# Top-k attention and gated feed-forward: scores split at 320 columns, attention areas in the outer banks, waits between different banks declared needless, feed-forward paced by section

## The chip, the cores and the metric

One core of one Trainium2 chip. The metric is the device time of the program in microseconds (us); the time before is the median of three runs. The profile comes from one further execution, and its span (first to last instruction of the program) is a little shorter than that execution's time.

The engines are named as in the profile: PE (TensorE matmuls) with PEld (its weight loads), DVE (VectorE), ACT (ScalarE), POOL (GpSimd), SP (SyncE, which here issues DMAs). Each runs its own queue in order, and an instruction waits on semaphores that other engines raise. PSUM, into which PE writes, is divided into banks of 512 fp32 columns for each of 128 partitions.

## The reference, cut to what matters

```python
def _attn_ref(q, k, v):                      # (8, 8, 576, 64) each
    scores = scale * np.matmul(q, k.transpose(0, 1, 3, 2))
    kth = np.partition(scores, -32, axis=-1)[..., -32:-31]
    scores = np.where(scores >= kth, scores, -1e9)
    attn = np.exp(scores - np.max(scores, axis=-1, keepdims=True))
    attn = attn / (np.sum(attn, axis=-1, keepdims=True) + 1e-09)
    return np.matmul(attn, v)

def _moe_ref(x, w_in, conv_w, w_out):        # x: (8, 576, 512), d_ff 1024
    h = np.maximum(x @ w_in, 0.0)
    conv_out = sum(conv_w[k] * hp[:, k:k + S, :] for k in range(3))   # hp: h padded by a row
    gate = 1.0 / (1.0 + np.exp(-conv_out))
    return h * gate @ w_out
```

## The kernel before, in words

The work is 288 tiles of 128 score rows by 576 columns. A batch has four pairs of heads; a pair has four full row blocks (one tile for each of its two heads) and a tail block in which the last 64 rows of both heads share a tile, so nine tiles, 36 a batch. The rows of a batch are done in two sections: section 0 takes two row blocks and the tail of every pair (20 tiles), section 1 the other two (16 tiles). When a section's attention is done, its feed-forward is queued and runs among the tiles of the next section: eight `Expand` units (x by w_in, each 12 matmuls, 258 columns wide for section 0 and 322 for section 1, L431), a convolution on POOL, a tanh on ACT, a gate on DVE, then `Contract` units (12 matmuls of 512 columns, L581).

`iteration(it)` records one step of a software pipeline, and each engine's queue is in that order (`manual_schedule`). On PE: four transposes of the weights of tile it-5 (L326), feed-forward matmuls (L431, L581) as a budget allows, a tail transpose (L339), the scores of a row block every second step (L241, or L229 for a tail block), and the products with v (`av`, L357 and L360). On ACT: relu of an expand (L445), the sign pass `sides` (L288), the copy of scores out of PSUM (`evacuate`, L248), the copy of an attention area (`av_out`, L368), the copy of the transposes (L331), the exponential of tile it-3 into `e_ps` (L300), and a tanh if there is one (L492). On DVE: seven partial maxima (L255), the merging of candidates (L275, L277), a maximum (L303), `select` (L307, tile `hot`), sometimes a gate (L500) and the row sums' inverses (L373, L374), and `weigh` (L313), which reads `e_ps`.

Two PSUM tiles matter. `s_ps` has three banks (columns 0 to 1535). The first head's scores stand from column `FIRST` = 64, the second's from `SECOND` = 896, so they reach over banks 0 and 1, and 1 and 2. A head's 576 columns are two matmuls cut at a bank boundary: `WIDE` = 448 for the first head. The two heads use different halves of PE's rows (64 partitions of q and k each). Call the four matmuls of a step A, B, C, D in the order of L235: A is 128 columns of head 0 (bank 1), B 448 of head 1 (bank 2), C 448 of head 0 (bank 0), D 128 of head 1 (bank 1). Before D stands a nop (L238) that waits for A, since both write bank 1. The two attention areas (`corner`) are columns 640 to 895, both in bank 1. `weights_ps` has two banks: `e_ps` (columns 0 to 575), `t_ps` (592 to 911, where the tanh goes), and in the last 32 columns the constants `above`, which `select` reads, and `sums_ps`, which the inverses write. The framework makes any two accesses from different engines to one PSUM tile wait for each other.

What sets the order of the feed-forward: `next_expand` hands out an expand when `state.it` has reached `state.due`, and then moves `due` on by `PACE` = 2.0 steps (L640 to L642); it also holds a section's expands back while contracts of the same section of an earlier batch have not been split.

Of the kernel before, what the change touches and what calls it, by code (L numbers as in the profile page):

```python
# [17 lines left out]
AF = mybir.ActivationFunctionType  # L18
ALU = mybir.AluOpType
ENG = mybir.EngineType  # L20

P = 128
# [31 lines left out]
OB = 1  # L54
WB = 256
FLIP_AT = 1.5
PACE = 2.0
STRIDE = 2
BANK = 512
SPB = 3  # L60
# [7 lines left out]
def attend_and_feed(ctx: ExitStack, tc: tile.TileContext, q, k, v, weights, out, shared, finish=None):  # L68
    nc = tc.nc
    exact = finish is None  # L70
    v_main, v_tail = v
    B, NPAIR, _, S = q.shape
    D = P // 2
    ident, wi, wo, cw, cr, kth, edge = shared
# [3 lines left out]
    SH = S // 2  # L78
    NI = S // P
    TAIL = S - NI * P  # L80
    FIRST, SECOND = TAIL, 3 * BANK - TAIL - S
    WIDE = BANK - FIRST
    MAIN = NI * P
    MIDDLE = NI // 2 * P
    NBLK = 2 * NI + 1
    scale = 1.0 / float(D) ** 0.5
    ROWS = [(0, NI * TAIL), (NI * TAIL, S)]
    SMAX = max(e - a for a, e in ROWS)
# [8 lines left out]
    dram = ctx.enter_context(tc.tile_pool(name="dram", bufs=2, space=bass.MemoryType.DRAM))  # L97

    weights_ps = ps.tile([P, 2 * BANK], F32, name="weights_ps", bufs=1)
    e_ps, t_ps = weights_ps[:, 0:S], weights_ps[:, S + 16:S + 16 + SMAX]  # L100
    above, sums_ps = weights_ps[:, 2 * BANK - 32:2 * BANK - 22], weights_ps[:, 2 * BANK - 16:2 * BANK - 16 + NBLK]
    for i in range(10):
        nc.vector.memset(above[:, i:i + 1], float(S - 2 * (TOPK - (i + 1 if i < 8 else 0))))
    rows = const.tile([P, XBUFS, S + 16], F32, name="rows")
# [14 lines left out]
    s_ps = ps.tile([P, 3 * BANK], F32, name="s_ps", bufs=1)  # L119
# [4 lines left out]
        return ps.tile([P, BANK], F32, name=name, tag=name, bufs=1)  # L124

    def corner(i):
        return s_ps[:, FIRST + S + i * P:FIRST + S + i * P + P]

    def warm_up(n):
        spare = bank("pt")  # L130
# [90 lines left out]
    def scores(t):  # L221
        kx, qx = t.pc.nat["k"], t.pc.nat["q"]
        i = t.j // 2
        rows_of = [slice(h * D, (h + 1) * D) for h in range(2)]
        if t.j == 2 * NI:
            for to, n in ((0, WIDE), (WIDE, MAIN - WIDE), (MAIN, TAIL)):
                for h, d in enumerate(rows_of):
                    at = (to + TAIL * h) % S
                    nc.tensor.matmul(s_ps[rows_of[1 - h], FIRST + to:FIRST + to + n], lhsT=qx[d, 0:TAIL], rhs=kx[d, at:at + n],  # L229
                                     start=True, stop=True)  # L230
        elif t.j % 2 == 0:
            c0 = i * P + (TAIL if t.pc.part == 0 else -MIDDLE)
            at = slice(c0, c0 + P)
            made = []
            for h, a, z in ((0, WIDE, S), (1, S - WIDE, S), (0, 0, WIDE), (1, 0, S - WIDE)):  # L235
                to = SECOND if h else FIRST
                if len(made) == 3:
                    tc.add_manual_dep(nc.tensor.nop().ins, made[0].ins.name,  # L238
                                      mybir.DependencyInfo(mybir.DependencyClass.Sync, mybir.DependencyReason.DATA),
                                      reason="two row tiles write one bank")  # L240
                made.append(nc.tensor.matmul(s_ps[:, to + a:to + z], lhsT=qx[rows_of[h], at], rhs=kx[rows_of[h], a:z],  # L241
                                             start=True, stop=True))

    def evacuate(t):
        t.row = rows[:, t.n % XBUFS]
        x = t.x = t.row[:, 8:S + 8]
        at = SECOND if t.j < 2 * NI and t.j % 2 else FIRST
        nc.scalar.copy(out=x, in_=s_ps[:, at:at + S])  # L248

    def chunk_ops(t):  # L250
        t.cand = att.tile([P, 8 * CHUNKS], F32, name="cand", bufs=4)
# [52 lines left out]

    def select(t):
        hot = att.tile([P, 10], F32, name="hot", bufs=3)
        nc.vector.scalar_tensor_tensor(out=hot, in0=above, scalar=t.cnt, in1=t.z[:, 0:10],  # L307
                                       op0=ALU.is_equal, op1=ALU.mult, accum_out=kth[:, t.n:t.n + 1])

    def weigh(t):  # L310
        if t.first:
# [37 lines left out]
    def av(st):  # L349
        w = st.w = P if st.i < NI else TAIL  # L350
        state.avs += 1
        a = st.a = corner(state.avs % 2)
        for i in range(NI + 1):
            for h in range(2):
                r = slice(h * D, (h + 1) * D)
                if i < NI:
                    nc.tensor.matmul(a[r, 0:w], lhsT=st.pc.vn[:, h, i], rhs=st.pT[:, h if st.i < NI else 1 - h, i, 0:w],  # L357
                                     start=(i == 0), stop=False)
                else:
                    nc.tensor.matmul(a[r, 0:w], lhsT=st.pc.vt[:, h], rhs=st.pTt[:, 0:w],  # L360
                                     start=False, stop=True)

    def av_out(st):
        pc = st.pc
        if st is pc.steps[0]:
            pc.xt = att.tile([P, MIDDLE + TAIL], F32, name="xt", bufs=2)
        c0 = pc.steps.index(st) * P
        nc.scalar.copy(out=pc.xt[:, c0:c0 + st.w], in_=st.a[:, 0:st.w])  # L368

    def inverses(pc):  # L370
        n = len(pc.blocks)
# [33 lines left out]
    class Expand:  # L405
# [82 lines left out]
        def tanh(self):  # L488
            alone = state.tanh_at < state.it and state.it < NT + 4 and not self.pooled()
            to = self.to = t_ps[:, 0:self.n] if alone else self.t  # L490
            state.tanh_at = state.it if alone else state.tanh_at
            nc.scalar.activation(out=to, in_=self.t, func=AF.Tanh,  # L492
                                 scale=1.0 if exact else cw[:, 1, self.f:self.f + 1])

        def pooled(self):
            return self.f == 0 and self.b < B - 1 and state.it < NT
# [138 lines left out]
    def next_expand():  # L635
        tail = state.it > NT + 4
        if not expands or expanded.waiting >= (4 if tail else EB) or state.blocks < 1 + NCT * DF // WB:
            return None
        e = expands[0]
        if any(o.part == e.part and o.b < e.b for o in unready) or (state.it < state.due and not tail):  # L640
            return None
        state.due = max(state.due + PACE, state.it - PACE)  # L642
        expanded.waiting += 1
        return expands.popleft()

# [10 lines left out]
    for b in range(B):  # L656
        for part in range(2):
            for g in range(NPAIR):
                pc = Box()
# [12 lines left out]
    state = Box()  # L672
# [5 lines left out]
    for lane, take in zip(lanes, (next_expand, next_contract)):  # L678
        lane.take, lane.cur, lane.waiting, lane.finished = take, None, 0, deque()
# [77 lines left out]
    def iteration(it):  # L757
# [32 lines left out]
        if pre is not None:  # L790
            evacuate(pre)
        outs, out_next = out_next, []
        for st in outs:
            av_out(st)
            if st is st.pc.steps[-1]:
                norm_wait.append((it + NORM_LAG, st.pc))
# [19 lines left out]
        for i in range(max(7, len(a_ops), len(b_ops))):  # L816
            if i < len(a_ops):
                a_ops[i]()
            for op in c_ops[i - 4:i - 3] if i > 3 else ():
                op()  # L820
            if tD is not None and not exact:
                if i == BELOW_AT:
                    below(tD)
                if i == BELOW_AT + 2:
                    select(tD)
            if i < len(b_ops):
                b_ops[i]()
            for op in r_ops[i - 5:i - 4] if i >= 5 else ():
                op()
# [35 lines left out]
        if n < NT:  # L865
            scores(tiles[n])
        for st in avs:
            av(st)
# [39 lines left out]
def kernel(  # L908
# [32 lines left out]
    def count_lost(total):  # L941
# [19 lines left out]
        nc.vector.tensor_copy(flag, total)  # L961

    attend_and_feed(tc, q, k, (v_main, v_tail), (w_in, conv_w, w_out), out, shared, count_lost)
    lost_rows = nc.values_load(flag[0:1, 0:1])
    with tc.If(lost_rows > 0):
        attend_and_feed(tc, q, k, (v_main, v_tail), None, out, shared)
# [56 lines left out]
```

## Time and profile before

| what | us |
|---|---|
| median of three runs (1082.56 to 1083.49) | 1083.39 |
| the profiled execution | 1083.43 |
| its span | 1081.6 |
| busy in the span: PE, DVE, ACT, POOL | 1005.6, 1007.5, 985.7, 920.8 |

The first 190 us also convert the weights; the last 66 us are feed-forward alone. Between them the four engines run side by side. A row of grouped instructions gives line, engine, operation, tiles out<-in, shapes, count, then busy us, mean ns of one, and idle us of the engine just before them with what ended it. A row of waits gives who waited for whom: us in total, times, the longest. A row of windows gives for a stretch its length and the busy time (and number) of PE, PEld, DVE, ACT and POOL, the granted clock, and the DMA share. A timeline row gives start, duration, engine, line, operation, tiles, shape, count.

### The profile page before, as it was taken

Reading aid. Unit: us, or ns where it says so; the run is one execution under the profiler, and the core shown is the slowest. Engines: PE = TensorE matmul, PEld = TensorE weight load, DVE = VectorE, ACT = ScalarE, POOL = GpSimd, SP = SyncE. Lnnn points to the kernel's source line nnn. Section 1 sums busy time; section 2 is a strip of 40 time slices with the busy share of each in tenths; the row PEclk is TensorE's granted clock in tenths of the full one; section 3 lists DMA queues with packets and bytes.
Section 4 is the critical chain, followed back from the end, with each engine's and each line's share of the span. In section 5 each row is a group of like instructions: output and inputs, shape, how many; then the busy total and the mean of one; then the engine's idle time right before and its main releaser. Section 6 shows DMA issues by size and latency. Waiting matters only on the chain.

```text
span 1081.6 us, 28860 instructions
## 1 busy us (share of the span) xinstructions
PE 1005.6 (93%) x8424; PEld 806.7 (75%) x8424; DVE 1007.5 (93%) x5816; ACT 985.7 (91%) x2374; POOL 920.8 (85%) x1203
## 2 busy tenths in 40 slices
PE   7766788899999999999999999999999999999997
PEld 5544656787788777878788777887888777887796
DVE  8999989999999999999999999999999999999752
ACT  6999998999999999999999989999999999999642
POOL 5899999999989799997889789997889879997800
PEclk8798989999999999999999999999999999999999
DMA  5343321222122213222222212222212222221101
GB/s 165 110 125 112 102 69 36 71 77 70 58 78 62 86 51 87 58 76 70 80 59 68 93 53 64 61 80 77 71 57 80 78 66 61 79 64 49 41 22 43
DMA packets 71302, 78.69 MB, mean 73 GB/s; under 512 B 12864, under 2 KB 46048, under 8 KB 71136
## 3 DMA queue, kind: packets, MB, share of 16 engines
q1 hardware_dynamic: 70992, 76.49, 23.8%
q8 instruction: 70, 1.15, 0.4%
q14 instruction: 96, 0.79, 0.2%
q10 hardware_dynamic: 144, 0.26, 0.1%
HBM read 67.13 MB, written 9.58 MB: 71 GB/s over the span
## 4 chain that ended last, share of the span: by engine, by line
PE 46%; DVE 30%; ACT 14%; POOL 6%; issue 3%; DMA 0%; SPq 0%; POOLq 0%; ACTq 0%
PE mc L581 10%; DVE cand L255 10%; PE me L431 9%; DVE e L313 7%; PE s_ps L357 7%; PE pt L326 7%; PE s_ps L241 6%; DVE z L303 5%; ACT weights_ps L300 3%; DVE cand L277 2%; ACT side L288 2%; ACT rows L248 2%; POOL z L293 2%; PE s_ps L229 2%; DVE rows L275 2%
## 5 line engine op out<-in xcount | busy, mean ns | idle before, releaser
L255 DVE MAX8 cand<-rows 128x8 f32<-128x82 f32 (+1 forms) x2016 | 456.8, 239 | 0.7 <-ACT rows L248 0.7
L293 POOL TENSOR_TENSOR z<-rows,side 128x579 f32<-128x579 f32 x288 | 347.7, 1207 | 66.1 <-ACT side L288 54.3
L431 PE MATMUL me<-x_hi,wi 128*128 128x258 f32 (+1 forms) x968 | 227.8, 308 | 2.3 <-ACT g L445 1.1
L313 DVE SCALAR_TENSOR_TENSOR e<-rows,kth,weights_ps 128x576 f32<-128x576 f32 x288 | 229.2, 796 | 0.1
L300 ACT ACTIVATE weights_ps<-rows,z 128x576 f32<-128x576 f32 x288 | 220.0, 764 | 8.5 <-DVE e L313 4.3
L288 ACT ACTIVATE side<-rows 128x576 bf16<-128x576 f32 x288 | 224.0, 778 | 0.4
L303 DVE MAX8 z<-z 128x8 f32<-128x576 f32 x288 | 213.8, 742 | 0.7 <-POOL z L293 0.7
L581 PE MATMUL mc<-wo,split 128*128 128x512 f32 x744 | 204.7, 406 | 3.1 <-POOL split L562 2.6
L248 ACT COPY rows<-s_ps 128x576 f32<-128x576 f32 x288 | 182.8, 635 | 26.0 <-PE s_ps L360 15.5
L326 PE MATMUL pt<-ident,e 128*128 128x128 f32 x1152 | 194.6, 293 | 4.1 <-ACT rT L381 3.0
L241 PE MATMUL s_ps<-k,q 64*128 64x448 f32 (+1 forms) x1024 | 165.3, 443 | 21.7 <-ACT xt L368 13.6
L357 PE MATMUL s_ps<-pT,vn 128*64 128x128 f32 (+1 forms) x2560 | 164.8, 272 | 14.3 <-ACT rows L248 13.7
L241 PEld LDWEIGHTS s_ps<-k,q 64*128 64x128 f32 x1024 | 117.5, 191 | 76.8 <-ACT xt L368 18.0
L431 PEld LDWEIGHTS me<-x_hi,wi 128*128 128x128 f32 x968 | 163.9, 189 | 4.8 <-ACT g L445 2.0
L357 PEld LDWEIGHTS s_ps<-pT,vn 128*64 128x64 f32 x2560 | 131.5, 139 | 46.8 <-ACT rows L248 22.7
L326 PEld LDWEIGHTS pt<-ident,e 128*128 128x128 f32 x1152 | 124.7, 144 | 42.5 <-issue 10.7
L331 ACT COPY pT<-pt 128x512 f32<-128x512 f32 x256 | 153.5, 600 | 2.8 <-PE pt L326 2.5
L581 PEld LDWEIGHTS mc<-wo,split 128*128 128x128 f32 x744 | 130.1, 189 | 25.9 <-POOL split L562 3.9
L431 PE MATMUL me<-x_lo,wi 128*128 128x258 f32 (+1 forms) x484 | 144.8, 299 | 0.0
L464 POOL TENSOR_SCALAR t<-g,cr 128x256 f32<-128x256 f32 (+1 forms) x234 | 119.4, 510 | 0.0
L275 DVE MAX8 rows<-cand 128x8 f32<-128x21 f32 x576 | 108.8, 189 | 0.0
L478 POOL TENSOR_TENSOR t<-t,t 128x256 f32<-128x256 f32 (+1 forms) x117 | 93.6, 800 | 9.7
(125 smaller groups left out, 1665.1 us busy)
## 6 DMA issues: line engine op xcount, KB each, us to landing
k<-in_k_dram SPq DMA_DIRECT2D x64, 288.0 KB
vn<-in_v_main_dram SPq DMA_DIRECT2D x64, 256.0 KB
rb<-row SPq DMA_DIRECT2D x128, 64.0 KB
out_dram<-o SPq DMA_DIRECT2D x26, 256.0 KB
q<-in_q_dram SPq DMA_DIRECT2D x31, 160.0 KB
raw<-in_w_in_dram SPq DMA_DIRECT2D x16, 256.0 KB
vt<-in_v_tail_dram SPq DMA_DIRECT2D x64, 64.0 KB
q<-in_q_dram SPq DMA_DIRECT2D x32, 128.0 KB
```

The source lines that it names most:

```text
L241: made.append(nc.tensor.matmul(s_ps[:, to + a:to + z], lhsT=qx[rows_of[h], at], rhs=kx[rows_of[h], a:z], start=True, stop=True))
L248: nc.scalar.copy(out=x, in_=s_ps[:, at:at + S])
L255: yield lambda c=c, at=at, n=n: nc.vector.max(out=t.cand[:, c:8 * CHUNKS:CHUNKS], in_=t.x[:, at:at + n])
L288: nc.scalar.activation(out=t.side[:, 2:S + 2], in_=t.x, func=AF.Sign, scale=-OVER, bias=t.row[:, 7:8], accum_out=t.cnt)
L293: nc.gpsimd.tensor_tensor(t.z[:, 8:S + 11], t.row[:, 6:S + 9], t.side, ALU.mult)
L300: nc.scalar.activation(out=e_ps, in_=t.x, func=AF.Exp, scale=scale, bias=t.shift)
L303: nc.vector.max(out=t.z[:, 0:8], in_=t.z[:, 10:S + 10])
L313: nc.vector.scalar_tensor_tensor(out=t.e, in0=t.x, scalar=kth[:, t.n:t.n + 1], in1=e_ps, op0=ALU.is_ge, op1=ALU.mult, accum_out=t.pc.sums[ ...
L326: nc.tensor.transpose(tp[:, i * P:(i + 1) * P], t.e[:, o + i * P:o + (i + 1) * P], ident)
L357: nc.tensor.matmul(a[r, 0:w], lhsT=st.pc.vn[:, h, i], rhs=st.pT[:, h if st.i < NI else 1 - h, i, 0:w], start=(i == 0), stop=False)
L431: nc.tensor.matmul(mm[:, 0:w], lhsT=wt, rhs=xx, start=(n == 0), stop=(n == len(ops) - 1))
L581: nc.tensor.matmul(mm[0:m], lhsT=x[:, i], rhs=wo[:, e, f], start=start, stop=stop)
```

## The change

`FIRST` becomes 192, so `SECOND` is 768 and `WIDE` 320: A is now 256 columns of head 0, B 320 of head 1, C 320 of head 0, D 256 of head 1, in the same banks as before. The tail block's pieces become 320, 192 and 64 columns in place of 448, 64 and 64. The attention areas go to columns 0 to 127 (bank 0) and 1408 to 1535 (bank 2), taken in turn. In `weights_ps`, `above` and `sums_ps` move to bank 0, `t_ps` to the end of bank 1; `e_ps` still reaches over both. A new function `apart` remembers the last 40 accesses to each of the two tiles that were passed to it and declares that two accesses from different engines to different banks do not depend on each other. It is applied to the scores, their copies, the products with v and their copies, and to `select` and the tanh. The pace of expands becomes 1.75 steps for section 0 and 2.5 for section 1.

```diff
-PACE = 2.0
+PACES = (1.75, 2.5)
...
-    FIRST, SECOND = TAIL, 3 * BANK - TAIL - S
+    FIRST = 192
+    SECOND = 3 * BANK - FIRST - S
...
-    e_ps, t_ps = weights_ps[:, 0:S], weights_ps[:, S + 16:S + 16 + SMAX]
-    above, sums_ps = weights_ps[:, 2 * BANK - 32:2 * BANK - 22], weights_ps[:, 2 * BANK - 16:2 * BANK - 16 + NBLK]
+    e_ps, t_ps = weights_ps[:, 2 * BANK - SMAX - S:2 * BANK - SMAX], weights_ps[:, 2 * BANK - SMAX:2 * BANK]
+    above, sums_ps = weights_ps[:, 0:10], weights_ps[:, 16:16 + NBLK]
...
-        return s_ps[:, FIRST + S + i * P:FIRST + S + i * P + P]
+        return s_ps[:, 3 * BANK - P:3 * BANK] if i else s_ps[:, 0:P]
+
+    recent = {nm: deque(maxlen=40) for nm in ("scores", "weights")}
+
+    def apart(inst, tile, first, last):
+        banks = range(first // BANK, (last - 1) // BANK + 1)
+        for other, theirs in recent[tile]:
+            if other.ins.engine != inst.ins.engine and not set(banks) & set(theirs):
+                tc.declare_no_dep(inst.ins, other.ins.name, reason="they use different PSUM banks")
+        recent[tile].append((inst, banks))
+        return inst
...
                 made.append(nc.tensor.matmul(s_ps[:, to + a:to + z], lhsT=qx[rows_of[h], at], rhs=kx[rows_of[h], a:z],
                                              start=True, stop=True))
+                apart(made[-1], "scores", to + a, to + z)
...
-        nc.scalar.copy(out=x, in_=s_ps[:, at:at + S])
+        apart(nc.scalar.copy(out=x, in_=s_ps[:, at:at + S]), "scores", at, at + S)
...
-        nc.vector.scalar_tensor_tensor(out=hot, in0=above, scalar=t.cnt, in1=t.z[:, 0:10],
-                                       op0=ALU.is_equal, op1=ALU.mult, accum_out=kth[:, t.n:t.n + 1])
+        apart(nc.vector.scalar_tensor_tensor(out=hot, in0=above, scalar=t.cnt, in1=t.z[:, 0:10], op0=ALU.is_equal,
+                                             op1=ALU.mult, accum_out=kth[:, t.n:t.n + 1]), "weights", 0, 1)
...
+            if alone:
+                apart(act, "weights", BANK, BANK + 1)
...
-        state.due = max(state.due + PACE, state.it - PACE)
+        state.due = max(state.due + PACES[e.part], state.it - PACES[e.part])
```

The first place is on PE, near the end of section 0 of batch 5: transposes of a tile (`pt`), feed-forward, the tail transpose (`me`), and a step of scores (A, B and C, D). A row's bracket names the semaphores on which it waits. Before:

```order
L326 MATMUL pt<-ident,e_12188 128x128 x3
L431 MATMUL me<-x_hi,wi 128x322
L431 MATMUL me<-x_lo,wi 128x322
L431 MATMUL me<-x_hi,wi 128x322
L581 MATMUL mc<-wo,split 128x512 x3
L339 MATMUL me<-ident,e_12188 128x128
L241 MATMUL s_ps<-k,q 128x128 [waits Activation_49]
L241 MATMUL s_ps<-k,q 128x448 x2
L241 MATMUL s_ps<-k,q 128x128 [waits PE_49]
```

and now:

```order
L339 MATMUL pt<-ident,e_12181 128x128 x3
L598 MATMUL mc<-wo,split 128x512 x2
L598 MATMUL mc<-wo,split 128x512 [waits Pool_49]
L598 MATMUL mc<-wo,split 128x512 x6
L352 MATMUL me<-ident,e_12181 128x128 [waits Activation_49]
L253 MATMUL s_ps<-k,q 128x256 [waits Activation_49]
L253 MATMUL s_ps<-k,q 128x320
L253 MATMUL s_ps<-k,q 128x320 [waits Activation_49]
L253 MATMUL s_ps<-k,q 128x256 [waits PE_49]
```

D still waits for A (PE_49), and A is twice as wide. The wait for the copy of an attention area has moved from A to C here (to B in the other half of the steps, when the area lies in bank 2). In place of six of the feed-forward matmuls stand nine contracts that came two tiles later before: counted between the transposes, section 0 of batch 5 held 120 expand and 51 contract matmuls and now holds 108 and 66, section 1 held 72 and 63 and now 84 and 54; in batches 4 and 6 the counts go from 120 and 57, 72 and 45 to 108 and 57, 84 and 39.

The second place is on DVE, at a step of an earlier batch in which a pair's row sums are inverted (`hot` is `select`, `sums` goes to `weights_ps`). Before:

```order
L307 SCALAR_TENSOR_TENSOR hot,kth<-weights_ps,cnt,z 128x10 [waits Activation_49]
L275 MAX rows<-cand 128x8 [waits DVE_49]
L255 MAX cand<-rows 128x8
L373 TENSOR_SCALAR weights_ps<-sums 128x5 [waits DVE_49]
L255 MAX cand<-rows 128x8
L374 RECIPROCAL rec<-weights_ps 128x5 [waits DVE_49]
```

and now:

```order
L320 SCALAR_TENSOR_TENSOR hot,kth<-weights_ps,cnt,z 128x10 [waits Activation_49]
L288 MAX rows<-cand 128x8 [waits DVE_49]
L268 MAX cand<-rows 128x8
L388 TENSOR_SCALAR weights_ps<-sums 128x5 [waits DVE_49,Activation_49]
L268 MAX cand<-rows 128x8
L389 RECIPROCAL rec<-weights_ps 128x5 [waits DVE_49]
```

`select` still waits for ACT, but for the exponential and no longer for the tanh behind it; the inverses' write, which `apart` does not cover, now waits for that tanh itself in 25 of 64 cases.

More of the change, by code (lines that the diff above doesn't have):

```diff
@@ L228, in scores @@
                     at = (to + TAIL * h) % S
-                    nc.tensor.matmul(s_ps[rows_of[1 - h], FIRST + to:FIRST + to + n], lhsT=qx[d, 0:TAIL], rhs=kx[d, at:at + n],
-                                     start=True, stop=True)
+                    mm = nc.tensor.matmul(s_ps[rows_of[1 - h], FIRST + to:FIRST + to + n], lhsT=qx[d, 0:TAIL],
+                                          rhs=kx[d, at:at + n], start=True, stop=True)
+                    apart(mm, "scores", FIRST + to, FIRST + to + n)
         elif t.j % 2 == 0:
@@ L352, in av @@
         a = st.a = corner(state.avs % 2)
+        st.at = 2 * BANK if state.avs % 2 else 0
         for i in range(NI + 1):
@@ L356, in av @@
                 if i < NI:
-                    nc.tensor.matmul(a[r, 0:w], lhsT=st.pc.vn[:, h, i], rhs=st.pT[:, h if st.i < NI else 1 - h, i, 0:w],
-                                     start=(i == 0), stop=False)
-                else:
-                    nc.tensor.matmul(a[r, 0:w], lhsT=st.pc.vt[:, h], rhs=st.pTt[:, 0:w],
-                                     start=False, stop=True)
+                    mm = nc.tensor.matmul(a[r, 0:w], lhsT=st.pc.vn[:, h, i],
+                                          rhs=st.pT[:, h if st.i < NI else 1 - h, i, 0:w], start=(i == 0), stop=False)
+                else:
+                    mm = nc.tensor.matmul(a[r, 0:w], lhsT=st.pc.vt[:, h], rhs=st.pTt[:, 0:w],
+                                          start=False, stop=True)
+                apart(mm, "scores", st.at, st.at + 1)
     def av_out(st):
@@ L367, in av_out @@
         c0 = pc.steps.index(st) * P
-        nc.scalar.copy(out=pc.xt[:, c0:c0 + st.w], in_=st.a[:, 0:st.w])
+        apart(nc.scalar.copy(out=pc.xt[:, c0:c0 + st.w], in_=st.a[:, 0:st.w]), "scores", st.at, st.at + 1)
     def inverses(pc):
@@ L491, in tanh @@
             state.tanh_at = state.it if alone else state.tanh_at
-            nc.scalar.activation(out=to, in_=self.t, func=AF.Tanh,
-                                 scale=1.0 if exact else cw[:, 1, self.f:self.f + 1])
+            act = nc.scalar.activation(out=to, in_=self.t, func=AF.Tanh,
+                                       scale=1.0 if exact else cw[:, 1, self.f:self.f + 1])
+            if alone:
+                apart(act, "weights", BANK, BANK + 1)
         def pooled(self):
```

## The prediction

> **What bounds the kernel now.** I read the shares of busy time first, then the waits, then the windows by section. The page's first row says only that everything is full:
>
> ```profile
> PE 1005.6 (93%) x8424; PEld 806.7 (75%) x8424; DVE 1007.5 (93%) x5816; ACT 985.7 (91%) x2374; POOL 920.8 (85%) x1203
> ```
>
> PE and DVE are level, ACT close behind. The waits that the change is about:
>
> ```profile
> DVE hot L307 <- ACT weights_ps L492: 21.0, 36, 1.6
> ...
> ACT rows L248 <- PE s_ps L360: 15.5, 30, 1.3
> PE s_ps L357 <- ACT rows L248: 13.7, 16, 1.5
> ...
> DVE hot L307 <- ACT weights_ps L300: 8.1, 15, 1.2
> ```
>
> `select` (hot) waits 21.0 us behind tanhs (L492) and 8.1 behind exponentials; PE and ACT wait for each other on `s_ps`. Whether such a wait is worth its length is read from the stretch in which it lies. I cut the loop where DVE's tiles change section; the rows are batch 0, the two sections of batch 1, of 5 and of 6, and the end of 7:
>
> ```profile
> core 0: us, PE busy (x) PEld busy (x) DVE busy (x) ACT busy (x) POOL busy (x), PEclk, DMA share, GB/s
> 17.60:146.70 129.10, 94.60 (x786) 70.32 (x786) 125.13 (x728) 124.50 (x318) 122.33 (x170) 0.85 0.34 105
> 146.70:219.40 72.70, 60.95 (x535) 48.76 (x536) 68.53 (x402) 67.99 (x170) 70.36 (x97) 0.93 0.19 53
> 219.40:273.80 54.40, 53.95 (x461) 43.60 (x460) 54.05 (x321) 52.19 (x126) 52.37 (x68) 1.00 0.26 79
> 648.00:717.60 69.60, 69.33 (x611) 56.16 (x608) 67.71 (x399) 66.93 (x164) 65.70 (x86) 1.00 0.22 62
> 717.60:772.70 55.10, 54.26 (x460) 43.40 (x459) 53.85 (x320) 52.65 (x126) 47.98 (x61) 1.00 0.29 83
> 772.70:841.80 69.10, 68.99 (x601) 56.13 (x599) 67.31 (x397) 66.79 (x162) 61.43 (x79) 1.00 0.22 63
> 841.80:897.10 55.30, 50.77 (x438) 40.24 (x438) 53.70 (x318) 51.66 (x123) 46.04 (x58) 1.00 0.26 78
> 966.60:1015.50 48.90, 46.75 (x397) 38.20 (x396) 45.26 (x251) 45.81 (x112) 41.99 (x53) 1.00 0.19 58
> ```
>
> From batch 2 on, section 0 leaves PE idle 0.27 us (odd batch) or 0.11 (even) of 69: PE is the bound there, though DVE is 97% busy, and DVE's 1.8 us of idleness are what it waits for PE's pace. Section 1 leaves PE 0.84 (odd) or 4.53 (even), and DVE, the busier or nearly so, 1.3 to 1.6. Batch 0 and section 0 of batch 1 leave PE over 11 us. So PE work costs in the first kind of stretch; a saved DVE wait pays in the others.
>
> **Term 1: the wait of D for A.** PE's instructions stay the same in number, and both heads still stream 576 columns, so by columns alone a step of scores keeps its length. But A grows from 128 to 256 columns, and D stands behind a nop that waits for A. One step before (the first matmul record alone, the first two, weight loads, the next work; then the nop and the means by shape):
>
> ```profile
> 303.51 0.37 PE L241 MATMUL s_ps<-k,q 64*128 64x128 f32 x1
> ...
> 303.51 0.65 PE L241 MATMUL s_ps<-k,q 64*128 64x128 f32 x2
> ...
> 303.73 0.30 PEld L241 LDWEIGHTS s_ps<-k,q 64*128 64x128 f32 x2
> ...
> 304.12 0.18 PEld L241 LDWEIGHTS s_ps<-k,q 64*128 64x128 f32 x1
> ...
> 304.38 0.19 PEld L241 LDWEIGHTS s_ps<-k,q 64*128 64x128 f32 x1
> ...
> 304.69 0.66 PE L326 MATMUL pt<-ident,e 128*128 128x128 f32 x4
> ...
> L238 PEldq EVENT_SEMAPHORE  x121: 51/51/51, 6.8 to 992.9; - x121
> ...
> L241 PE MATMUL s_ps<-k,q 64*128 64x448 f32 x512 | 163.9, 582 | 0.0
> ...
> L241 PE MATMUL s_ps<-k,q 64*128 64x128 f32 x512 | 114.3, 304 | 21.7 <-ACT xt L368 13.6 <-ACT rows L248 7.9
> ```
>
> A step takes 304.69 - 303.51 = 1.18 us. Each fp32 matmul leaves two records (1024 for 128 steps of four). The second record is over after 0.65, longer than a 128-wide one lasts: it is B, which starts beside A. So the heads run side by side. A column costs a record (582 - 304) / 320 = 0.87 ns, so 128 more columns of a matmul cost 2 x 128 x 0.87 = 0.22 us.
>
> C's two weight loads end at 304.03, D's first starts at 304.12, 0.61 after the step began. In nearly every step (121 times) L238 stands as a wait of its own ahead of it. I take it that D's load comes when A is done. That cost nothing: D had to wait for B's 448 columns anyway, and began about where its second load stands, at 304.38 (0.87 in). From there to the step's end it took 0.31.
>
> Now A ends 0.22 later, and D's load comes at 0.83. From the second load that a half gets to its matmul is some 0.11 (the first loads stand about that far apart: 303.51, then 303.73 for C, two a half), so D begins at 0.94, where B, 0.22 shorter, would have let it begin at 0.65. D's columns end the step at 0.94 + 0.31 + 0.22 = 1.47: **0.29 us longer, I take 0.28**. The bounds are 0 (D's load is not tied to A's end) and 0.29. Sixteen steps a batch are 4.5 us of PE, 36 us in all; each section gets 8 x 0.28 = 2.24.
>
> What of that ends on the path is what PE's idle time does not hold. Batches 2 to 7, section 0: 2.0 (odd), 2.1 (even), three of each, 12.3. Section 1: odd 1.4, in batches 3 and 5, 2.8; even 0; the last 0. Batch 1: section 0 none, section 1 2.24 - 0.45 = 1.8. Batch 0 none. **Together +16.9.**
>
> **Term 2: `select` without the tanh.** The tanh stands right behind the exponential on ACT. A wait falls by at most the tanh's time:
>
> ```profile
> L492 ACT ACTIVATE weights_ps<-t,cw 128x256 f32<-128x256 f32 (+1 forms) x101 | 50.9, 504 | 3.1 <-DVE e L313 0.4
> ```
>
> At most 36 x 0.504 = 18.1 of the 21.0; many are shorter than a tanh, so three quarters, 16. It is kept where PE is not the bound. Rows of L307 by stretch (batch 1 section 0, batch 2 section 1, the last):
>
> ```profile
> L307 DVE SCALAR_TENSOR_TENSOR hot<-weights_ps,cnt,z 128x10 f32<-128x10 f32 x20 | 4.3, 217 | 3.5 <-ACT weights_ps L492 3.3 <-ACT weights_ps L300 0.2
> L307 DVE SCALAR_TENSOR_TENSOR hot<-weights_ps,cnt,z 128x10 f32<-128x10 f32 x16 | 3.4, 214 | 1.3 <-ACT weights_ps L492 1.0 <-ACT weights_ps L300 0.3
> L307 DVE SCALAR_TENSOR_TENSOR hot<-weights_ps,cnt,z 128x10 f32<-128x10 f32 x15 | 3.3, 217 | 3.4 <-ACT weights_ps L492 2.9 <-ACT weights_ps L300 0.5
> ```
>
> Three quarters of 3.3, two thirds of 1.0 in each of three even batches, and half of 2.9 (three long waits): 2.5 + 2.0 + 1.5, **-6.0**. The new wait of the inverses for the tanh comes a merge and a partial maximum later on DVE; behind it are a reciprocal, the gate (which needs the tanh too) and `weigh`. At most what is left of the longest waits, some 25 x 0.1; it goes with the quarter that I don't count.
>
> **Term 3: the other bank waits.** From the build, copies of scores that wait for a product with v fall from 131 to 85, products that wait for such a copy from 86 to 70, and the 62 steps that waited for an area's copy at A now wait at B or C, at most a third of a microsecond later. Their cost now is the last two rows on `s_ps` among the waits, and the 13.6 and 7.9 us behind L241's 128-wide matmuls. Where PE is the bound it had at most 0.3 us idle to give back, and elsewhere DVE sets the pace: between 0 and -3, taken **-1**.
>
> **Term 4: pace.** A contract matmul costs 1.40 / 6 = 0.233 us, an expand's 1.44 / 12 = 0.12 (258 wide):
>
> ```profile
> 641.32 1.44 PE me L431 x12
> ...
> 645.88 1.40 PE mc L581 x6
> ```
>
> Section 0 gets 12 expand matmuls less and, in odd batches, 15 contracts more: +2.1 odd, -1.4 even, where PE is full both times; net +0.7 a pair. Much of it is nine contracts moved over the border by a tile or two, so between -4 (evener load) and +6 (the odd sections alone), taken **+1**. After the last transposes 121 expand and 159 contract matmuls remain in place of 132 and 148: 11 x (0.233 - 0.12) = **+1.2**, on a tail that PE sets. A split moves there from POOL to DVE, which has room.
>
> **Term 5: carry-over.** PE may fall behind by about a step, so a part of what section 0 of an even batch gains in length can be worked off in section 1, which has 4.5 - 2.2 us left: **-3** (1 in each of three), between 0 and -6.
>
> Sum: 16.9 - 6.0 - 1.0 + 1.0 + 1.2 - 3.0 = +9.1, on the profiled execution's 1083.43, which lies 0.04 from the median. **1092 us**, 0.8% slower.
>
> **The rivals.** *No longer step.* D's load was late for another reason, or a wide A ends sooner than its columns say. Then Term 1 and 5 go, and a little more of the tanhs counts: batch 1 section 1 0.3, odd sections 1 0.84 twice, full sections 0.2 six times, 3.2: -6.0 - 3.2 - 1.0 + 1.0 + 1.2 = -8, 1075. For it: the row shows only that D's load is late, not for whom, and the 29 us of waits at L307 are real. Against it: the constant nop.
>
> *Matmuls in program order.* If each record starts only after the one before has started, B would stand behind A's second. With 0.39 for 448 columns, 0.28 for 320, 0.22 for 256 and 0.11 for 128, C would end the old step at 0.89 + 0.39 = 1.28 and D the new at 1.00 + 0.22 = 1.22: 0.06 less, 0.5 a section, and 1071. Against it the second record, which is B's. The Trainium skill's page PSUM — Partial Sum Buffer, section Engine vs sequencer instructions, says that matmuls start and complete in program order; for the two heads' halves this case's trace does not agree (0.65 after the start two records are over, and one of them is 448 wide).
>
> *Absorbed.* PE's busy rows overlap, so its full sections may hold waits that I don't see, into which the longer step goes: with 1.0 in place of 2.0 a full section, 1086; with none, 1080.
>
> *Overload.* Nothing is worked off later and the odd sections keep their 2.1 us of feed-forward: 16.9 - 6.0 + 6.3 + 1.2 = +18, 1101.
>
> **How the numbers follow.** The forecast (1087 to 1097) 0.47, absorbed 0.23 (half of it slower, the rest within 0.2%), no longer step 0.16, program order 0.04, overload 0.10. A measurement of this kernel tells 0.2%, 2.2 us, from no change. Faster 0.21 (with a little of the absorbed), same 0.12, slower 0.67. The range, 1074 to 1100, takes in the case without a longer step and reaches nearly to the overload.
>
> **What would show it.** Right: a step of scores of 1.44 to 1.47 us from its first matmul to the next work, D's weight load some 0.83 in; waits of `select` for the tanh gone, those for the exponential near 8 or fewer; sections 0 of batches 2 to 7 at 71 to 72 us with PE idle under 0.5. Wrong: a step of 1.18. If the step is longer and the time is not, PE's work was not the bound in section 0.

## The result, and the profile after

| | us, median | lowest to highest | runs |
|---|---|---|---|
| before | 1082.79 | 1081.82 to 1083.49 | 5 |
| after | 1097.95 | 1097.56 to 1101.67 | 5 |

The runs before are the three from ahead of the prediction and two more. The ratio is 1.0147, with a 95% interval of 1.0129 to 1.0164: the changed kernel is 14 to 18 us slower. The execution that was profiled took 1097.70, its span 1095.9. In the changed kernel the lines have moved: the scores are L253 (L241 before) and their nop L250 (L238), `select` is L320 (L307), the exponential L313 (L300), the tanh L507 (L492), the copy of scores L261 (L248).

The first row of the page after (busy time, share of the span, instructions of each engine) and its row of the chain of work that ended last:

```profile
PE 1027.8 (94%) x8424; PEld 818.7 (75%) x8424; DVE 1012.8 (92%) x5817; ACT 990.2 (90%) x2374; POOL 920.5 (84%) x1202
...
PE 68%; DVE 19%; ACT 9%; POOL 2%; issue 1%; ACTq 0%; POOLq 0%
```

The shares of busy time hardly move. The chain does; this is the same row of the page before:

```profile
PE 46%; DVE 30%; ACT 14%; POOL 6%; issue 3%; DMA 0%; SPq 0%; POOLq 0%; ACTq 0%
```

PE has taken the chain over, half of it from DVE. What makes PE later is seen in one step of scores. From the timeline of after (start, length, operation): the first matmul record, the first two, the second weight load of C, the first of D, and the next work:

```profile
331.49 0.48 PE L253 MATMUL s_ps<-k,q 64*128 64x256 f32 x1
...
331.49 0.54 PE L253 MATMUL s_ps<-k,q 64*128 64x256 f32 x2
...
332.03 0.19 PEld L253 LDWEIGHTS s_ps<-k,q 64*128 64x128 f32 x1
...
332.31 0.18 PEld L253 LDWEIGHTS s_ps<-k,q 64*128 64x128 f32 x1
...
332.93 0.33 PE L339 MATMUL pt<-ident,e 128*128 128x128 f32 x1
```

D's load comes 332.31 - 331.49 = 0.82 into the step (0.61 before), and the step takes 332.93 - 331.49 = 1.44 us (1.18 before). Nanoseconds of the same records give 1.443 against 1.174, 0.269 more, the median of all 128 steps: 128 x 0.269 = 34.4 us of PE. The tail blocks, whose pieces changed too, are not longer: their step has a median of 1.126 us, before 1.131. The waits of after (engine, line waited for, us, times, longest):

```profile
DVE hot L320 <- ACT weights_ps L313: 35.0, 67, 1.3
...
ACT rows L261 <- PE s_ps L374: 15.0, 25, 1.2
ACT rows L261 <- PE s_ps L253: 14.4, 25, 2.2
...
PE s_ps L371 <- ACT rows L261: 7.0, 9, 1.9
```

The waits of `select` for the tanh (21.0 us) are gone, and those for the exponential are up from 8.1 to 35.0: more than both together before. The windows of after, cut where the tiles change section: batch 0, the two sections of batch 1, of 5 and of 6, the end of 7:

```profile
core 0: us, PE busy (x) PEld busy (x) DVE busy (x) ACT busy (x) POOL busy (x), PEclk, DMA share, GB/s
17.60:145.00 127.40, 91.41 (x786) 67.48 (x786) 125.16 (x728) 123.75 (x319) 121.19 (x168) 0.92 0.34 107
145.00:219.50 74.50, 60.26 (x521) 47.39 (x522) 68.76 (x401) 68.11 (x168) 72.08 (x100) 0.91 0.18 51
219.50:274.80 55.30, 55.30 (x446) 44.05 (x447) 53.92 (x318) 52.29 (x123) 47.34 (x59) 1.00 0.26 78
655.00:727.40 72.40, 72.40 (x603) 57.67 (x598) 67.99 (x398) 67.64 (x164) 63.80 (x82) 1.00 0.21 63
727.40:783.00 55.60, 55.60 (x466) 44.66 (x467) 54.10 (x320) 52.38 (x125) 48.70 (x63) 1.00 0.24 78
783.00:853.90 70.90, 70.17 (x591) 55.87 (x588) 67.90 (x398) 66.92 (x159) 62.68 (x79) 1.00 0.20 61
853.90:908.50 54.60, 52.81 (x451) 42.26 (x451) 53.73 (x319) 52.03 (x125) 45.99 (x59) 1.00 0.27 79
980.90:1030.10 49.20, 48.07 (x401) 38.77 (x400) 45.64 (x250) 45.50 (x111) 42.57 (x55) 1.00 0.17 52
```

Section 0 is 2.8 us longer in batch 5 and 1.8 in batch 6, and PE is without idle time in three of these rows. Section 0 of batch 1, where I counted a gain, is 1.8 longer, and section 1 of batch 6, where PE had 4.5 us to spare, only 0.7 shorter.

### The profile page after: what moved, and what is told of

Its sections match the earlier page's. It is cut to its first block, busy times and chain, and to the rows that moved or that the text cites. A ratio compares the mean times of both kernels' runs of the same rounds, so it can differ in the third digit from the quotient of the medians.

```text
span 1095.9 us, 28858 instructions
## 1 busy us (share of the span) xinstructions
PE 1027.8 (94%) x8424; PEld 818.7 (75%) x8424; DVE 1012.8 (92%) x5817; ACT 990.2 (90%) x2374; POOL 920.5 (84%) x1202
## 4 chain that ended last, share of the span: by engine, by line
PE 68%; DVE 19%; ACT 9%; POOL 2%; issue 1%; ACTq 0%; POOLq 0%
PE mc L598 15%; PE me L446 13%; PE s_ps L253 11%; PE pt L339 10%; PE s_ps L371 9%; DVE cand L268 6%; DVE e L326 4%; DVE z L316 3%; PE s_ps L240 2%; ACT weights_ps L313 2%; PE s_ps L374 2%; DVE cand L290 2%; PE weights_ps L598 2%; ACT side L301 2%; ACT rows L261 1%
## 5 line engine op out<-in xcount | busy, mean ns | idle before, releaser
L313 ACT ACTIVATE weights_ps<-rows,z 128x576 f32<-128x576 f32 x288 | 220.3, 765 | 1.9 <-DVE e L326 1.5
L253 PE MATMUL s_ps<-k,q 64*128 64x320 f32 (+1 forms) x1024 | 198.4, 449 | 22.9 <-ACT rows L261 22.8
L261 ACT COPY rows<-s_ps 128x576 f32<-128x576 f32 x288 | 182.9, 636 | 31.4 <-PE s_ps L374 15.0
L598 PE MATMUL mc<-wo,split 128*128 128x512 f32 x732 | 200.1, 405 | 1.8 <-POOL split L579 0.9
L339 PE MATMUL pt<-ident,e 128*128 128x128 f32 x1152 | 192.2, 290 | 3.8 <-ACT rT L396 2.4
L253 PEld LDWEIGHTS s_ps<-k,q 64*128 64x128 f32 x1024 | 127.5, 190 | 72.1 <-ACT rows L261 27.8
```

The lines of the kernel that those rows point to most:

```text
L261: apart(nc.scalar.copy(out=x, in_=s_ps[:, at:at + S]), "scores", at, at + S)
L313: nc.scalar.activation(out=e_ps, in_=t.x, func=AF.Exp, scale=scale, bias=t.shift)
L339: nc.tensor.transpose(tp[:, i * P:(i + 1) * P], t.e[:, o + i * P:o + (i + 1) * P], ident)
L598: nc.tensor.matmul(mm[0:m], lhsT=x[:, i], rhs=wo[:, e, f], start=start, stop=stop)
```

## The experiments

The theory to test is that D's wait for a wider A makes the step longer and PE hands that on (T). The rivals, as the trace of after suggests them: the moved feed-forward (R1; the odd sections 0 grew most), and new waits on `weights_ps` (R2; the waits of `select` for the exponential grew). All times are medians of three or five rounds beside the kernel before, in three groups of runs and a last one; "us" in the table is (ratio - 1) x 1082.5.

| kernel | step, us | median | ratio (95%) | us |
|---|---|---|---|---|
| after | 1.443 | 1097.95 | 1.0147 (1.0129 to 1.0164) | +15.9 |
| after, FIRST = 128 | 1.229 | 1084.87 | 1.0022 (1.0012 to 1.0031) | +2.4 |
| after, one pace | 1.44 | 1102.01 | 1.0185 (1.0168 to 1.0202) | +20.0 |
| after, weights as before | 1.44 | 1102.80 | 1.0181 (1.0164 to 1.0198) | +19.6 |
| after, scores not declared | 1.44 | 1098.84 | 1.0157 (1.0140 to 1.0174) | +17.0 |
| before + areas | 1.443 | 1102.07 | 1.0177 (1.0162 to 1.0193) | +19.2 |
| before + weights | 1.174 | 1079.75 | 0.9969 (0.9958 to 0.9980) | -3.4 |
| before + paces | 1.17 | 1083.12 | 1.0006 (0.9996 to 1.0015) | +0.6 |
| before + weights + paces | 1.17 | 1079.84 | 0.9975 (0.9965 to 0.9986) | -2.7 |
| before, D waits for B | 1.559 | 1115.55 | 1.0313 (1.0291 to 1.0334) | +33.9 |
| the same + paces | 1.56 | 1110.16 | 1.0268 (1.0243 to 1.0293) | +29.0 |
| after, unequal areas | 1.171 | 1080.71 | 0.9984 (0.9975 to 0.9993) | -1.7 |
| before + weights + paces from batch 1 | 1.17 | 1080.32 | 0.9981 (0.9972 to 0.9990) | -2.1 |

**A shorter A.** The changed kernel with 192 columns for A in place of 256.

```diff
-    FIRST = 192
+    FIRST = 128
```

> The changed kernel with FIRST = 128 in place of 192: A and D are 192 columns wide, B and C 384; everything else of the change stays (areas, declarations, paces). Theory T (the longer step of scores is the cause: D waits for A, and A is wide): A ends 64 x 2 x 0.87 ns = 0.11 us earlier than in the changed kernel, D's weight load comes about 0.71 into the step in place of 0.81, D's columns are 0.11 shorter, so the step is 1.23 to 1.27 us in place of 1.44; that takes 0.2 x 8 = 1.6 us off each section, and the kernel to 1083 to 1088. Rival R1 (the moved feed-forward is the cause) and rival R2 (new waits on the two banks of weights_ps are the cause): both stay as they are, so 1095 to 1098, with the step shorter and PE idle instead.

From the timeline of this kernel, the start of a step, D's load and the next work:

```profile
331.61 0.59 PE L253 MATMUL s_ps<-k,q 64*128 64x192 f32 x2
...
332.31 0.18 PEld L253 LDWEIGHTS s_ps<-k,q 64*128 64x128 f32 x1
...
332.84 0.33 PE L339 MATMUL pt<-ident,e 128*128 128x128 f32 x1
```

D's load 0.70 in, the step 1.23, and 13.5 of the 15.9 us are gone. One number of the source, which changes no declaration, no pace and nothing on `weights_ps`, takes nearly all of the loss back. R1 and R2 as causes fall here: the step is short again, and paces and `weights_ps` are still those of the change.

**The layout of weights_ps alone**, in the kernel before.

```diff
-    e_ps, t_ps = weights_ps[:, 0:S], weights_ps[:, S + 16:S + 16 + SMAX]
-    above, sums_ps = weights_ps[:, 2 * BANK - 32:2 * BANK - 22], weights_ps[:, 2 * BANK - 16:2 * BANK - 16 + NBLK]
+    e_ps, t_ps = weights_ps[:, 2 * BANK - SMAX - S:2 * BANK - SMAX], weights_ps[:, 2 * BANK - SMAX:2 * BANK]
+    above, sums_ps = weights_ps[:, 0:10], weights_ps[:, 16:16 + NBLK]
...
+        apart(nc.vector.scalar_tensor_tensor(out=hot, in0=above, scalar=t.cnt, in1=t.z[:, 0:10], op0=ALU.is_equal,
+                                             op1=ALU.mult, accum_out=kth[:, t.n:t.n + 1]), "weights", 0, 1)
...
+            if alone:
+                apart(act, "weights", BANK, BANK + 1)
```

> The kernel before, with only the new layout of weights_ps and the declaration for select and the tanh. My term 2: waits of select for the tanh (21.0 us) go, 6 us of them on the path: 1076 to 1078. Rival R2 (select waits for the exponential instead, which stands right ahead of the tanh on ACT; the inverses get a wait for the tanh): waits of select for the exponential rise from 8.1 to 25 or more, and the time is 1082 to 1085. If R2 is what makes the changed kernel slow, 1088 or more.

The waits of `select` in this kernel (its lines: `select` L317, the exponential L310):

```profile
DVE hot L317 <- ACT weights_ps L310: 22.3, 46, 1.5
```

The wait for the tanh is gone, and 22.3 us for the exponential stand where 21.0 + 8.1 = 29.1 stood for both. So 6.8 us of waiting are saved where I counted 16, and 3.4 of the time where I counted 6: between the two expectations. The trace shows where the rest went, when the waits are compared tile by tile (288 tiles in the same order in both kernels). The 36 tiles that waited for a tanh keep 7.3 of their 21.0 us: 13.7 went, not far from the 16. The 15 that waited for an exponential have 9.0 in place of 8.1. And 16 tiles that did not wait before now wait 6.0 us, because DVE now gets there before ACT's exponential is over. The other side of the new layout, the write of the inverses, which may now wait for a tanh, costs nothing: DVE never sat idle before it (L383 here, L388 in after).

**The paces alone**, in the kernel before, and **one pace** in the changed kernel.

```diff
-PACE = 2.0
+PACES = (1.75, 2.5)
...
-        state.due = max(state.due + PACE, state.it - PACE)
+        state.due = max(state.due + PACES[e.part], state.it - PACES[e.part])
```

> The kernel before, with only PACES (1.75, 2.5) in place of PACE 2.0. My term 4 with the tail: +2.2, so 1084 to 1086. Rival R1 (the moved feed-forward makes the odd batches' section 0 longer by what it brings): +5 to +8, 1088 to 1091, with section 0 of odd batches 1.5 us or more longer and PE full there. If the paces serve what they seem made for (an evener load), 1079 to 1082.

```diff
-PACES = (1.75, 2.5)
+PACES = (2.0, 2.0)
```

> The changed kernel with both paces 2.0. Theory T: the step stays at 1.44 us and the time within 3 us of the changed kernel, 1094 to 1099. Rival R1: the kernel goes back to 1088 to 1092, with section 0 of odd batches some 1.5 us shorter.

Alone they change nothing that can be measured. In the changed kernel, going back to one pace costs 4.1 us. That is outside what either theory expected, and against R1: the moved feed-forward does not make the changed kernel slow, it relieves it. Batches 5 and 6 with one pace:

```profile
656.60:727.30 70.70, 70.59 (x605) 56.80 (x600) 68.12 (x399) 66.90 (x163) 65.28 (x85) 1.00 0.22 61
727.30:784.30 57.00, 56.45 (x460) 44.45 (x459) 54.47 (x319) 52.66 (x124) 48.27 (x61) 1.00 0.27 80
784.30:855.40 71.10, 70.99 (x602) 57.37 (x599) 67.97 (x397) 66.94 (x162) 60.98 (x77) 1.00 0.21 61
855.40:911.70 56.30, 53.19 (x443) 41.63 (x442) 53.84 (x319) 52.31 (x125) 46.41 (x60) 1.00 0.25 76
```

With two paces the odd section 0 is 1.7 longer (72.4), but both sections 1 are shorter, by 1.4 and 1.7, and the even section 0 by 0.2: 253.5 in place of 255.1 for the pair. It is the second sections, which I had left out of the term, that pay.

**D waits for B**, in the kernel before: the step made longer by a wait alone, with nothing else of the change.

```diff
-                    tc.add_manual_dep(nc.tensor.nop().ins, made[0].ins.name,
+                    tc.add_manual_dep(nc.tensor.nop().ins, made[1].ins.name,
```

> The kernel before, and D's nop waits for B in place of A; split, areas, declarations and paces as before, so the only thing that changes is how late D starts. B's record ends 1.02 us into the step, the semaphore is seen 0.04 later, D's load stands 0.075 behind that at 1.14 in place of 0.60, and the step is 1.50 to 1.60 us in place of 1.17: 0.33 to 0.43 more, where the changed kernel has 0.27 more. Theory T (the length of the step is the price, as in term 1 of the prediction): 0.39 x 8 = 3.1 us a section, of which the full sections hold nothing back: 3.0 x 6 + 2.3 x 2 + 2.6 = 25, so 1102 to 1110. If the length of the step is not what the changed kernel pays for (it pays for the areas, the declarations or the paces), 1083 to 1092, with PE waiting elsewhere less.

A step of this kernel, from its timeline:

```profile
332.63 0.65 PE L241 MATMUL s_ps<-k,q 64*128 64x128 f32 x2
...
333.77 0.18 PEld L241 LDWEIGHTS s_ps<-k,q 64*128 64x128 f32 x1 [0.63 <-issue]
...
334.19 0.44 PE L326 MATMUL pt<-ident,e 128*128 128x128 f32 x2
```

Its waits of `select` (L307; L492 the tanh, L300 the exponential):

```profile
DVE hot L307 <- ACT weights_ps L492: 34.5, 59, 1.5
...
DVE hot L307 <- ACT weights_ps L300: 18.2, 34, 1.8
```

The waits of its ACT for PE, at the copy of scores (L248):

```profile
ACT rows L248 <- PE s_ps L360: 24.4, 33, 1.8
ACT rows L248 <- PE s_ps L241: 22.4, 37, 2.3
```

And its windows of the two sections of batch 6:

```profile
793.50:865.70 72.20, 72.09 (x598) 55.26 (x597) 67.94 (x398) 67.45 (x161) 61.70 (x78) 1.00 0.20 60
865.70:922.20 56.50, 53.37 (x437) 39.97 (x439) 53.74 (x318) 51.62 (x123) 45.84 (x59) 1.00 0.26 76
```

D's load is where it was expected, 1.14 in, and the step 0.385 longer: 49 us of PE, of which 33.9 reach the end. That is above the range, which went by the 25 that my way of counting gives. The full section 0 grew by 72.2 - 69.1 = 3.1, all of 8 x 0.385, but section 1 grew too, by 1.2, with 3.1 us of PE idle in it. The waits of `select` rise from 29.1 to 52.7 us although nothing on `weights_ps` was touched: they are how a late PE shows on DVE, by way of ACT, whose own waits for PE at the copy of scores rise from 15.5 + 9.3 = 24.8 to 46.8 us. So the 35.0 us in the profile of after are a symptom of the step, and not the cause that R2 takes them for.

**Weights and paces together**, without the areas (the diffs of these two parts above):

> The kernel before with the two parts that leave the step of scores alone: the new layout of weights_ps with its declarations, and PACES (1.75, 2.5). Additive (weights alone gave -2.9, paces alone +0.5): 1079 to 1081.5. If the paces pay once DVE waits less (with the long step, going back to one pace cost 4 us): 1075 to 1079. If the odd sections are overloaded with the new paces: 1082 to 1085.

Additive, 0.9975: the two parts that leave the step of scores alone make a kernel that is 0.2 to 0.3% faster than before.

**The changed kernel with one part taken back**, first the declarations on `s_ps` (every `apart(..., "scores", ...)` is left out), then the layout of `weights_ps` (the diff of above, reversed).

> The changed kernel without the declarations on s_ps (scores, copies, products with v): the areas, the split, weights_ps and the paces stay, and an instruction on s_ps may again wait for one on another bank. Term 3 (they are worth about 1 us, at most 3): 1098 to 1101. If they are worth a lot, hidden behind the longer step: 1103 or more. If they do harm (work of PE let through early collides with other work): 1092 to 1096.

> The changed kernel with weights_ps laid out and waited for as before (the tanh wait of select is back); split, areas, declarations on s_ps and paces stay. Theory T with PE as the bound (term 2 gave little in the changed kernel because PE sets the pace in more of it): 1097 to 1100, with waits of select for the tanh near 20 us and those for the exponential near 10. If term 2 is worth as much here as alone (2.9 us) or more: 1100.5 to 1104. Rival R2 (the new layout does harm in the changed kernel): 1090 to 1096.

The declarations are worth 1.1 us, as term 3 said, though the intervals overlap. The layout of `weights_ps` is worth 3.7: as much as alone, and no harm. The waits of `select` in that kernel (L507 the tanh, L313 the exponential) are 32.3 + 12.0 = 44.3 us, against 35.0 in the changed one:

```profile
DVE hot L320 <- ACT weights_ps L507: 32.3, 46, 1.7
...
DVE hot L320 <- ACT weights_ps L313: 12.0, 28, 1.0
```

**The areas alone**, in the kernel before: only the split at 320 columns and the areas in the outer banks.

```diff
-    FIRST, SECOND = TAIL, 3 * BANK - TAIL - S
+    FIRST = 192
+    SECOND = 3 * BANK - FIRST - S
...
-        return s_ps[:, FIRST + S + i * P:FIRST + S + i * P + P]
+        return s_ps[:, 3 * BANK - P:3 * BANK] if i else s_ps[:, 0:P]
```

> The kernel before with only the split at 320 columns and the areas in the outer banks (FIRST = 192); no declarations, weights_ps and pace as before. If the parts add up, it is the changed kernel (+15) less what each other part gave in it: weights 4.9, paces 4.1, declarations 0.9: 1105 to 1110. That is, 34 us of PE from 128 longer steps would cost some 25, two thirds, as 49 us cost 33 where D waits for B. By my term 1 with the carry-over (+13.9): 1095 to 1099; then the parts do not add up, and the other parts only do something together.

+19.2: this part alone is slower than the whole change. It missed both expectations. The parts do not add up: taken away from the changed kernel, weights, paces and declarations cost 3.7, 4.1 and 1.1, together 8.9, but all three added to the areas bring 3.3. The areas alone, the changed kernel with one pace and the one with the old weights all stand within 0.8 us of each other (+19.2, +20.0, +19.6): with the long step, the layout without the paces brings nothing, nor do the paces without the layout. Why they need each other no run here shows.

**The paces with another long step**: D waits for B, and PACES (1.75, 2.5).

> D waits for B (step 1.56 us, as in the run of that name) and PACES (1.75, 2.5). If the paces pay because the steps are longer (4 us in the changed kernel, nothing with the short step): 1109 to 1113, with the second sections of even batches 1 to 1.5 us shorter. If they pay only with the areas or the declarations of the changed kernel: 1114 to 1118.

4.9 us less than the same step with one pace, though the ends of the two intervals touch, and section 1 of batch 6 is 55.1 us long in place of 56.5, as expected. So the paces can pay with no areas, no declarations and the old layout about. That a long step is enough for it is not shown: in the changed kernel with the old layout the step is long too, and there they bring nothing (+19.6, the areas alone +19.2).

**The whole change with a short step.** The areas start at 64 and 832, so A is 128 columns again, C 448, B 384 and D 192; one attention area lies between them, in bank 1, the other in bank 2.

```diff
-    FIRST = 192
-    SECOND = 3 * BANK - FIRST - S
+    FIRST = 64
+    SECOND = 3 * BANK - P - S
...
-        return s_ps[:, 3 * BANK - P:3 * BANK] if i else s_ps[:, 0:P]
+        return s_ps[:, 3 * BANK - P:3 * BANK] if i else s_ps[:, FIRST + S:FIRST + S + P]
...
-            for h, a, z in ((0, WIDE, S), (1, S - WIDE, S), (0, 0, WIDE), (1, 0, S - WIDE)):
+            for h, a, z in ((0, WIDE, S), (1, 2 * BANK - SECOND, S), (0, 0, WIDE), (1, 0, 2 * BANK - SECOND)):
```

> The changed kernel with areas of unequal split: the first at column 64, the second at 832, one area of the attention output between them, the other at 1408. A is 128 columns wide again and C 448, B is 384 and D 192. Theory T: D's load comes at 0.60 into the step as before, D's columns then end with C's at 1.17 to 1.20 us, and with the weights, the paces and the declarations of the change the kernel is at 1077 to 1081, below the kernel before and near the best part alone (1079.8). If the step is not what counts: 1090 or more.

The start of a step, D's load and the next work, from the timeline:

```profile
331.23 0.59 PE L253 MATMUL s_ps<-k,q 64*128 64x128 f32 x2
...
331.83 0.18 PEld L253 LDWEIGHTS s_ps<-k,q 64*128 64x128 f32 x1
...
332.40 0.66 PE L339 MATMUL pt<-ident,e 128*128 128x128 f32 x4
```

The waits of its `select`:

```profile
DVE hot L320 <- ACT weights_ps L313: 23.4, 47, 1.0
```

Its windows of the sections of batches 5 and 6:

```profile
647.90:718.40 70.50, 70.50 (x606) 56.67 (x603) 67.64 (x398) 67.35 (x164) 63.71 (x83) 1.00 0.22 65
718.40:772.40 54.00, 53.66 (x463) 43.23 (x463) 53.75 (x320) 51.92 (x125) 47.93 (x62) 1.00 0.27 80
772.40:841.60 69.20, 68.15 (x593) 54.52 (x590) 67.49 (x398) 66.48 (x160) 62.98 (x80) 1.00 0.21 62
841.60:895.70 54.10, 50.92 (x448) 41.22 (x450) 53.70 (x320) 51.81 (x125) 45.87 (x60) 1.00 0.27 80
```

D's load is back at 0.60, the step at 1.17, `select` waits 23.4 us in place of 35.0, and the kernel is a little faster than before. This is the cleanest comparison: layout of `weights_ps` and paces are those of the change, and the declarations apply. Against it the changed kernel pays +15.9 + 1.7 = 17.6 us for its long step (with what the place of one attention area does to it).

**A version to beat them all**: weights, and the two paces only for batches 1 to 7.

```diff
-        state.due = max(state.due + PACES[e.part], state.it - PACES[e.part])
+        pace = PACES[e.part] if e.b else 2.0
+        state.due = max(state.due + pace, state.it - pace)
```

> A version that should beat both: the kernel before with the new weights_ps and its declarations (alone 1079.8), and the two paces only for the feed-forward of batches 1 to 7, with 2.0 for that of batch 0. With weights and both paces throughout, section 0 of batch 1 took 75.5 us against 73.0 with weights alone, and the pairs of later sections 1.5 to 2 less. If the 2.5 us hang on the pace: 1076.5 to 1078.5, with section 0 of batch 1 at 73 and the rest as with both paces. If section 0 of batch 1 is longer for something else (where the first feed-forward falls among the loads): 1079 to 1081.

A miss. In its profile section 0 of batch 1 did fall from 75.5 to 72.2 us, but over the twelve runs nothing is left of it: 0.9981, not to be told from weights alone or weights with both paces. What stands in batches 0 and 1 of a single profile is a poor guide here, since the granted clock there differs from run to run (0.91 and 0.93 in that section of these two profiles; more below). Weights alone has the lowest ratio, 0.9969.

## Why the prediction was right, and where its sum was off

**The mechanism of term 1** is shown. The prediction has D's load at 0.83 and a step of 1.44 to 1.47; the trace has 0.82 and 1.443 in after. The step can be moved by the length of A (FIRST = 128, the unequal areas) and by the wait alone (D waits for B), and the time moves with it each time. Of the other signs that the prediction names, one failed outright: waits of `select` for the exponential near 8 us, where 35.0 came. PE's idle time in section 0 of batch 6 is 0.7 us, a little over the 0.5 named, and section 0 of batch 5, at 72.4, a little over the 72.

**The size of term 1 without the carry-over** held: +16.9 forecast, 17.6 between the changed kernel and the one with unequal areas (with the carry-over, which the 17.6 contains, 13.9 was forecast). By sections, from the windows of these two (us that the long step adds):

| section | forecast | measured |
|---|---|---|
| batch 5, section 0 | 2.0 | 72.4 - 70.5 = 1.9 |
| batch 5, section 1 | 1.4 | 55.6 - 54.0 = 1.6 |
| batch 6, section 0 | 2.1 | 70.9 - 69.2 = 1.7 |
| batch 6, section 1 | 0, and -1 by term 5 | 54.6 - 54.1 = +0.5 |

**Term 5, the carry-over (-3), failed.** It took PE's idle time in the even sections 1 for room in which work can be caught up. There the short-step kernel left PE 54.10 - 50.92 = 3.2 us idle, the changed one 1.8, and the section still became 0.5 longer. So most of the longer steps there went into idle time (1.4 us of it), but not all, and nothing was caught up: a sum of idle time over a section does not tell what lies where. Where D waits for B it shows again, in the 1.2 us of section 1 of batch 6; I had put these sections at nothing there too.

**Term 2 (-6) was mis-sized**: 3.4 alone and 3.7 in the changed kernel. The step of it that failed is not so much the "three quarters" of the wait for the tanh, since 13.7 of the 21.0 us did go at the tiles that had it. It is that nothing was put down for new waits: with the layout alone, 6.9 us of waits for the exponential came up, most of them at tiles that had not waited, so that 6.8 of 29.1 us were saved in all.

**Terms 3 and 4** are small and were taken small. Term 3 (-1): 1.1 measured, within its error. Term 4 with the tail (+2.2): +0.6 with the short step, but -4.1 with the long one, so the sign was wrong in the kernel that it was meant for. It priced PE's rows of section 0 (+2.1 odd, -1.4 even; +1.7 and -0.2 measured) and left out sections 1, where the gain is (-1.4 and -1.7). The +1.2 on the tail did not show either: the last stretch, after the sections, took 65.8 us, before 66.1 (granted clock 0.99 and 0.97). Why a section 1 that holds more of PE's matmuls (451 in place of 443 in batch 6) becomes shorter, the runs do not settle.

**In sum**, +9.1 was forecast and +15.9 measured. Of the 6.8 between them, 3.0 are term 5, 3.1 the terms 2 to 4 (-6.0 - 1.0 + 2.2 = -4.8 forecast, -1.7 measured with the short step) and 0.7 term 1. Of the 3.1, term 2 brought 2.6 less than forecast and the paces cost 1.6 less; the other 2.1 lie with the declarations and the moved areas, and differences of this size are near the noise. The measured 1097.95 lies inside the range (1074 to 1100), but just above the band of the forecast itself (1087 to 1097): the direction and the main term were right, and the size came out low.

**The rivals.** No longer step, matmuls in program order, and absorbed are out: the step is longer, and it costs half or more of its length (17.6 of 34.4 us). For the program order the single records decide, two to a matmul. That two of them overlap, as the prediction argued, does not go against an order of starts. But where D waits for B, the record that raises D's semaphore is B's second, and it begins 0.49 us into the step, after C's first at 0.33, though C stands behind B in PE's queue. The Trainium skill's page PSUM — Partial Sum Buffer, section Engine vs sequencer instructions, says that matmuls start and complete in program order; for single records of the two heads' halves this trace does not agree. Taken whole, the four matmuls of that step do begin and end in their order: A 0 to 0.49, B 0.01 to 1.02, C 0.33 to 1.24, D 1.17 to 1.63.

Overload (1101) was near in size, and half right: nothing was worked off later, as it said, but it also had the paces load the odd sections, and they relieve the changed kernel by 4.

## What to carry to other kernels

Before a tile is split at another column, follow which matmul waits for which on a shared bank: here the length of the first of four decided when the last could begin, and 128 columns moved from one to another, at an unchanged total, cost 17.6 us, 1.6% of the kernel. When a wait grows in the profile after, ask whether its own code changed: `select` waited longest for an exponential, and the cause was a matmul two engines away, which only a run with nothing but that matmul's wait changed could show. And do not price a removed wait by its own length: here DVE, set free of the tanh, met 6.9 us of new waits for the exponential, most of them at other tiles.

## What the runs showed of the hardware

The semaphore between the two halves of PE's rows cost nearly the same each time. The nop stands as a row of its own in 121 of 128 steps (L250 of after, from the view of its line: durations, first and last start):

```profile
L250 PEldq EVENT_SEMAPHORE  x121: 51/51/51, 6.6 to 1007.9; - x121
```

It starts 0.042 to 0.045 us after the recorded end of the matmul that it waits for, at all 121 places in each of three kernels; in the steps shown above: before (0.485, then 0.527 into the step), after (0.696 and 0.738), D waits for B (1.023 and 1.065). D's weight load follows 0.075 to 0.077 us behind in these steps. In the seven steps without that row, D's load came 0.06 earlier, and with FIRST = 128 the step was 1.171 in place of 1.229.

The granted clock of the two profiles differs at the start, while the rows shown from section 1 of batch 1 on all stand at 1.00: in batch 0 it is 0.85 before and 0.92 after, with 94.60 and 91.41 us of PE for the same 786 matmuls, and in section 0 of batch 1 0.93 and 0.91. A difference of two or three microseconds in batches 0 and 1 of two single profiles is no finding.
